# An order of issue written by hand, one broadcast product for four heads, and scores in column halves: one core of a Trainium2

## The chip, the cores and the metric

The kernel runs on one core of one Trainium2 chip. The time is the device time of one execution in microseconds (us), the median of the runs shown. Engines are named as in the profile: PE (TensorE, matrix products; PEld its loads of the stationary operand), DVE (VectorE), ACT (ScalarE), POOL (GpSimd), SP (SyncE, which here issues nearly all transfers).

## The reference, cut to what matters

Three parts follow each other: a gated linear attention over 768 steps for 4 batches of 8 heads with head dimension 40, then two feed-forward layers 320 -> 2048 -> 320 on the 3072 tokens.

```python
for t in range(S):                       # attention, per batch and head
    m_new = np.maximum(f_gate[:, :, t] + m, i_gate[:, :, t])
    f_stab = np.exp(f_gate[:, :, t] + m - m_new)
    i_stab = np.exp(i_gate[:, :, t] - m_new)
    m = m_new
    C = f_stab * C + i_stab * outer(vt, kt)
    n = f_stab * n + i_stab * kt
    y[:, :, t] = sigmoid(o_gate[:, :, t]) * (C @ qt) / max(abs(n @ qt), 1)
x = y, heads side by side                # 3072 x 320
x = relu(x @ w_in) ** 2 @ w_out          # layer 0
return elu(x @ w2_in) @ w2_out           # layer 1, elu(h) = h if h > 0 else exp(h) - 1
```

## The kernel before

The attention is computed in 6 chunks of 128 steps. A unit u is one chunk of one batch (24 in all), and n counts half units of four heads (48 in all). Within a chunk the weights of step s for step t are `exp(a_s - max_t)`, where `a` is the running gate term and `max` its running maximum; scores times these weights give P, and P times the values gives the output. For later chunks the maximum is stored to memory and read back as a broadcast (`mb_load`), masked on POOL (`mask`) and put through the exponential with `a` as the bias (`emit_E`, one ACT instruction for each head). For the first chunk (n = 0 to 7) the whole exponent is built on PE by `m_pe`: one product puts in the causal mask (`identr` by `negmask`), one for each head broadcasts minus the maximum over the 128 rows (a column of the identity `sel`, repeated by a zero step, by `nst`), and one adds `a` (`ast` by `sel`, repeated). `e0` takes the exponential of the 128x512 result in one ACT instruction. Numbers in `nst` and `ast` are held in 64 rows, a high and a low part of 32 rows each, one row for each batch and head.

Scores: `s_pe` for n = 0 to 7 multiplies 40 rows (the head dimension), `scores` does it for the other n; for n = 8 to 15 its operands are plain fp32 with 120 rows, of which 80 are zeros (n < `NPLAIN` = 16), for later n an fp32r form in 120 rows. `emit_P` multiplies with the weights on DVE. `columns` splits a product into two, over the first and last 64 columns of the stationary operand, which write PSUM partitions 0 to 63 and 64 to 127; `pv0` and `values` use it for the values. `state_sum` adds up the state. `evac0`/`evac`, `norm`, `trans`, `x_hi`, `x_lo` bring the output into X, the input of layer 0, for four units at a time.

A weight tile f (16 for each layer) arrives as `raw` and is turned into a high and a low fp32r part by `w_scale`, `w_low`, `w_hi` on ACT and `w_shift`, `w_sign`, `w_add`, `w_lo` on DVE. One step of a layer is one tile of 128 hidden columns for 512 tokens: `mm1` (8 products into h, line 492), `elem` (ACT) and `elem_lo` (DVE), `mm2` (8 products into acc, line 536).

The order of the first part is written out by hand: the string `ORDER` is a list of words, a letter for the task and a number, and each engine gets its instructions in just this order (`manual_schedule`). The letters: Q scores' operands, K keys, values and output gate, q, B, R (weight tile), G, r are loads; m, e, s, p, v, z are maximum's term, exponential, scores, P, values and their copy for n = 0 to 7; k, o, n, t, h, l are the weighting of the keys, the output gate, norm, transposes and the two parts of X for each unit; b, c, d, f, a, H, L are the seven steps of a weight tile (scale, low, shift, sign, add, high part, low part); M, E, S, V, Z, y, Y are the attention of the later chunks; 1, A, F, 2, 3 are the steps of layer 0 (mm1, elem, elem_lo, the first five and the last three products of mm2); g, x, C, U, D are the gates. `i3` puts three products of 512 columns into `dps` (line 657), whose result is never read; 20 of them stand before everything else. With step 20 the string ends and a loop goes on for the rest. `h` has two PSUM buffers; PE's products of `m_pe` use them too.

Of the kernel before, what the change touches and what calls it, by code (L numbers as in the profile page):

```python
# [6 lines left out]
F32 = mybir.dt.float32  # L7
F32R = mybir.dt.float32r
# [32 lines left out]


ORDER = """
R0 Q0 G1 K0 Q1 Q2 K1 Q3 R1 R2 Q4 K2 c0 Q5 Q6 b0 K3 s0 Q7 g1 q4 Q9 m0 o0 k0 K4 Q8 i2 m1 d0 e0 D1 f0 G2 x1 K5 m2
p0 R3 e1 k1 q5 a0 o1 i1 v0 Q11 e2 Q10 H0 i2 m3 r0 z0 G3 L0 i1 m4 c1 e3 i1 s2 b1 e4 i1 m5 p2 b2 d1 i2 v2 f1 e5
d2 R4 i1 m6 o2 k2 z2 a1 f2 i1 m7 H1 c2 L1 i2 s4 e6 k3 R5 a2 o3 i2 s1 p4 H2 L2 i3 v4 p1 i4 s3 o4 B8 B10 B12 i2
v1 p3 o5 i4 s5 B9 z1 n0 c3 i2 v3 p5 b3 z4 i1 t0 z3 d3 i4 s7 e7 n1 h0 l0 i2 s6 p7 b4 f3 i1 C1 i4 v5 p6 R6 U1 a3
k4 b5 i2 t1 k5 B11 z5 d4 M8 H3 n2 i1 v7 h1 E8 i3 v6 l1 M12 c4 f4 M9 i3 t2 B14 E12 z7 M10 R7 z6 d5 i2 S8 n3 h2
E9 Q12 l2 i3 t3 M11 f5 h3 M14 E10 l3 i2 10 a4 E11 g2 11 c5 L3 A0 D2 R8 a5 12 p8 A1 F0 13 b6 F1 c6 S9 d6 f6 H4
20 Q13 H5 p9 R9 30 L4 A2 V4 a6 L5 q6 c7 B16 F2 B13 14 b7 B15 Z4 b8 H6 S10 x2 d8 E14 21 Q14 L6 M16 f8 31 b9 M13  # L50
22 n4 A3 15 d9 K6 M15 A4 d7 f9 16 f7 E13 F3 R10 a7 32 E15 t4 p10 23 k6 F4 H7 33 A5 L7 24 17 c8 F5 h4 R11 a8
b10 l4 34 H8 d10 25 c9 L8 A6 R12 35 f10 18 a9 A7 F6 S11 26 Q15 p11 c10 F7 H9 R13 36 a10 b11 V5 L9 c11 q7 d11
b12 B17 Z5 19 A8 n5 H10 27 o6 A9 37 L10 K7 t5 M17 110 F8 f11 b13 d12 h5 R14 28 a11 f12 H11 C2 38 k7 d13 c12 29
L11 A10 R15 a12 111 f13 c13 U2 F9 S12 H12 a13 b14 39 Q16 p12 c14 210 d14 l5 H13 S13 L12 A11 112 L13 F10 b15
p13 310 o7 d15 A12 V6 F11 f15 q8 f14 B18 y16 113 Z6 E17 E16 211 a14 A13 311 M18 n6 S14 212 Q17 p14 c15 K8 F13
H14 S15 F12 E18 L14 t6 312 p15 h6 114 l6 a15 y17 Y16 V7 H15 k8 A14 q9 L15 Q18 B19 115 Z7 o8 213 n7 A15 313 S16
F14 K9 t7 p16 214 y18 M19 F15 h7 Y17 314 E19 215 l7 Q19 116 Y18 o9 k9 g3 Q20 117 A16 D3 118 A17 F16 119 x3 S17
315 y19 p17 V8 F17 P15 Y19 216 Z8 Q21 B20 A18 120 B21 q10 n8 316 S18 K10 F18 t8 y20 217 p18 h8 Y20 S19 A19 317
M20 121 p19 Q22 l8 M21 y21 F19 E20 V9 Y21 q11 B22 Z9 Q23 218 B23 A20 318 n9 C3 219 A21 U3 K11 319 F20 S20 p20
F21  # L60
"""


def body(tc, qk, qp, kvo, gates, wq, ident_in, qkm_in, out):
# [28 lines left out]
    ident = constp.tile([128, 128], F32, name="ident")  # L93
    msk = constp.tile([128, 1], F32, name="msk")
    msk2 = constp.tile([64, 1], F32, name="msk2")
    sel = constp.tile([64, 32], F32R, name="sel")
    qkm = constp.tile([3 * D, 2], F32, name="qkm")
    one = constp.tile([64, 1], F32, name="one")
    dve.memset(msk[0:64], 0.0)
# [757 lines left out]
```

## Time and profile before

| | |
|---|---|
| median of 3 runs | 836.69 us (836.54 to 837.39) |
| the profiled execution, its own time | 834.66 us |
| its span on the engines | 832.8 us |
| busy: PE, DVE, ACT, POOL | 820.8, 558.4, 543.8, 119.3 us |

Times in the views are counted from the start of the span. The profiled execution is one of its own; its time lies 2.03 us under the median of the runs.

### The profile page before, as it was taken

Reading aid. Unit: us, or ns where it says so; the run is one execution under the profiler, and the core shown is the slowest. Engines: PE = TensorE matmul, PEld = TensorE weight load, DVE = VectorE, ACT = ScalarE, POOL = GpSimd, SP = SyncE. Lnnn points to the kernel's source line nnn. Section 1 sums busy time; section 2 is a strip of 40 time slices with the busy share of each in tenths; the row PEclk is TensorE's granted clock in tenths of the full one; section 3 lists DMA queues with packets and bytes.
Section 4 is the critical chain, followed back from the end, with each engine's and each line's share of the span. In section 5 each row is a group of like instructions: output and inputs, shape, how many; then the busy total and the mean of one; then the engine's idle time right before and its main releaser. Section 6 shows DMA issues by size and latency. Waiting matters only on the chain.

```text
span 832.8 us, 14363 instructions
## 1 busy us (share of the span) xinstructions
PE 820.8 (99%) x5349; PEld 693.3 (83%) x5349; DVE 558.4 (67%) x995; ACT 543.8 (65%) x1012; POOL 119.3 (14%) x195
## 2 busy tenths in 40 slices
PE   9999999999999999999999999999999999999997
PEld 5668788788888888888888879999999899999996
DVE  5799997766667666655449975665655665655554
ACT  5589886766776776678479974555644644655543
POOL 4031101211111111000000011111111111111111
PEclk9999999999999999999999999999999999999999
DMA  8845645754655534561235420110200200000000
GB/s 267 269 140 190 201 129 151 243 153 138 177 137 167 150 110 145 148 190 31 86 101 196 140 89 1 37 47 1 83 1 1 83 1 1 33 1 0 32 1 33
DMA packets 32668, 85.39 MB, mean 103 GB/s; under 512 B 4087, under 2 KB 7895, under 8 KB 32599
## 3 DMA queue, kind: packets, MB, share of 16 engines
q1 hardware_dynamic: 32311, 84.15, 33.2%
q8 instruction: 42, 0.69, 0.4%
q10 hardware_dynamic: 288, 0.33, 0.1%
q14 instruction: 27, 0.22, 0.1%
HBM read 75.73 MB, written 8.73 MB: 101 GB/s over the span
## 4 chain that ended last, share of the span: by engine, by line
PE 84%; ACT 6%; DVE 5%; issue 3%; DMA 2%; POOL 0%; POOLq 0%; DVEq 0%; ACTq 0%; SPq 0%
PE h L492 37%; PE acc L536 35%; PE dps L657 2%; PE pv L323 2%; PE s L312 2%; PE in L323 1%; ACT ct L122 1%; ACT w L144 1%; ACT cu L127 1%; ACT ghi L505 1%; PE in L380 1%; ACT r L504 1%; DVE w L150 1%; ACT r L506 1%; DMA rqk<-qk 1%
## 5 line engine op out<-in xcount | busy, mean ns | idle before, releaser
L492 PE MATMUL h<-xh,w 128*128 128x512 f32 x1152 | 357.8, 393 | 0.4
L492 PEld LDWEIGHTS h<-xh,w 128*128 128x128 f32 x1152 | 216.2, 188 | 46.0 <-DVE w L150 0.8
L520 DVE TENSOR_TENSOR glo<-r,ghi 128x512 fp32r<-128x512 f32 x192 | 135.3, 705 | 161.0 <-ACT r L506 84.6
L536 PE MATMUL acc<-w,ghi 128*128 128x320 f32 x768 | 170.2, 308 | 1.2 <-POOL ghi L515 0.6
L510 ACT ACTIVATE r<-h 128x512 f32<-128x512 f32 x96 | 57.6, 600 | 153.7 <-PE h L492 152.2
L492 PE MATMUL h<-xl,w 128*128 128x512 f32 x384 | 150.9, 393 | 0.2 <-DVE xl L397 0.2
L536 PEld LDWEIGHTS acc<-w,ghi 128*128 128x128 f32 x768 | 132.3, 188 | 9.0 <-POOL ghi L515 0.9
L536 PE MATMUL acc<-ghi,w 128*128 128x512 f32 x480 | 128.2, 396 | 0.0
L536 PE MATMUL acc<-w,glo 128*128 128x320 f32 x384 | 118.8, 309 | 0.2 <-DVE glo L520 0.2
L515 POOL TENSOR_SCALAR ghi<-r 128x512 fp32r<-128x512 f32 x96 | 60.4, 629 | 356.3 <-DVE r L514 263.8
L513 DVE SCALAR_TENSOR_TENSOR ex<-ex,th 128x512 f32<-128x512 f32 x96 | 66.4, 692 | 52.0 <-ACT ex L512 51.4
L536 PEld LDWEIGHTS acc<-ghi,w 128*128 128x128 f32 x480 | 87.2, 188 | 16.8 <-ACT y L563 0.3
L505 ACT ACTIVATE ghi<-r 128x512 fp32r<-128x512 f32 x96 | 60.7, 632 | 47.2 <-PE acc L536 46.3
L536 PE MATMUL acc<-glo,w 128*128 128x512 f32 x288 | 81.7, 392 | 2.1 <-DVE glo L520 2.1
L504 ACT ACTIVATE r<-h 128x512 f32<-128x512 f32 x96 | 56.6, 589 | 40.4 <-PE h L492 40.3
L492 PEld LDWEIGHTS h<-xl,w 128*128 128x128 f32 x384 | 72.1, 188 | 11.4 <-DVE xl L397 0.6
L536 PEld LDWEIGHTS acc<-w,glo 128*128 128x128 f32 x384 | 72.1, 188 | 0.4 <-DVE glo L520 0.4
L514 DVE SCALAR_TENSOR_TENSOR r<-h,ex 128x512 f32<-128x512 f32 x96 | 66.3, 691 | 3.1
L536 PEld LDWEIGHTS acc<-glo,w 128*128 128x128 f32 x288 | 53.6, 188 | 13.7 <-DVE glo L520 2.5
L511 ACT ACTIVATE th<-r 128x512 f32<-128x512 f32 x96 | 61.0, 635 | 2.7
L506 ACT ACTIVATE r<-r 128x512 f32<-128x512 f32 x96 | 60.7, 632 | 2.6
L512 ACT ACTIVATE ex<-r 128x512 f32<-128x512 f32 x96 | 59.2, 616 | 0.0
(104 smaller groups left out, 857.4 us busy)
## 6 DMA issues: line engine op xcount, KB each, us to landing
raw<-wq SPq DMA_DIRECT2D x32, 704.0 KB, 5.5
rqk<-qk SPq DMA_DIRECT2D x32, 480.0 KB, 8.1
kvo<-kvo SPq DMA_DIRECT2D x24, 488.0 KB, 6.7
mb<-negm_dr SPq DMA_DIRECT2D x40, 256.0 KB, 4.0
qp<-qp SPq DMA_DIRECT2D x20, 256.0 KB, 5.6
y_dr<-y SPq DMA_DIRECT2D x18, 256.0 KB, 2.9
out<-y SPq DMA_DIRECT2D x22, 160.0 KB, 1.8
yr<-y_dr SPq DMA_DIRECT2D x12, 256.0 KB, 3.1
```

Source lines behind the costliest of these rows:

```text
L492: lambda i=i, a=a, b_=b_: pe.matmul(h[:, 0:n], lhsT=a, rhs=b_, start=(i == 0), stop=(i == len(seq) - 1))
L504: act.activation(out=r, in_=h, func=AF.Relu)
L505: act.activation(out=hi, in_=r, func=AF.Square)
L506: act.activation(out=r, in_=r, func=AF.Square)
L510: act.activation(out=r, in_=h, func=AF.Relu, scale=-1.0)
L511: act.activation(out=th, in_=r, func=AF.Tanh, scale=0.5)
L512: act.activation(out=ex, in_=r, func=AF.Exp, scale=-1.0)
L513: dve.scalar_tensor_tensor(out=ex, in0=ex, scalar=1.0, in1=th, op0=ALU.add, op1=ALU.mult)
L514: dve.scalar_tensor_tensor(out=r, in0=h, scalar=0.0, in1=ex, op0=ALU.max, op1=ALU.subtract)
L515: pool_.tensor_scalar(out=hi, in0=r, scalar1=1.0, scalar2=1.0, op0=ALU.mult, op1=ALU.mult)
L520: dve.tensor_tensor(out=lo, in0=r, in1=hi.bitcast(F32), op=ALU.subtract)
L536: ops.append(lambda: pe.matmul(o, lhsT=l_, rhs=r_, start=first and st, stop=last and sp_))
```

## The change

Four things are changed. `m_pe`'s four products of 128 columns and 64 rows become one of 512 columns and 128 rows: its moving operand `nst4` holds minus the maximum of all heads in 4 blocks of 128 columns, with zeros where a row's head is not the one of that block, and its stationary operand `selq` picks the four rows of n; `ast` and `sel` get 128 rows too, the lower 64 of them zeros. `nst4` and `selq` are prepared once, with two reductions, a copy and a multiply on DVE and two memsets on POOL. The scores of the first two chunks (n = 0 to 15) go through `columns`. The fillers ahead are 17, not 20. The order is a new one: the tasks are the same, and the fillers in it are 33, not 59. The diff, with the two orders up to somewhat past the first step of layer 0 (word `10`):

```diff
@@ -41,23 +41,22 @@
 ORDER = """
-R0 Q0 G1 K0 Q1 Q2 K1 Q3 R1 R2 Q4 K2 c0 Q5 Q6 b0 K3 s0 Q7 g1 q4 Q9 m0 o0 k0 K4 Q8 i2 m1 d0 e0 D1 f0 G2 x1 K5 m2
-p0 R3 e1 k1 q5 a0 o1 i1 v0 Q11 e2 Q10 H0 i2 m3 r0 z0 G3 L0 i1 m4 c1 e3 i1 s2 b1 e4 i1 m5 p2 b2 d1 i2 v2 f1 e5
-d2 R4 i1 m6 o2 k2 z2 a1 f2 i1 m7 H1 c2 L1 i2 s4 e6 k3 R5 a2 o3 i2 s1 p4 H2 L2 i3 v4 p1 i4 s3 o4 B8 B10 B12 i2
-v1 p3 o5 i4 s5 B9 z1 n0 c3 i2 v3 p5 b3 z4 i1 t0 z3 d3 i4 s7 e7 n1 h0 l0 i2 s6 p7 b4 f3 i1 C1 i4 v5 p6 R6 U1 a3
-k4 b5 i2 t1 k5 B11 z5 d4 M8 H3 n2 i1 v7 h1 E8 i3 v6 l1 M12 c4 f4 M9 i3 t2 B14 E12 z7 M10 R7 z6 d5 i2 S8 n3 h2
-E9 Q12 l2 i3 t3 M11 f5 h3 M14 E10 l3 i2 10 a4 E11 g2 11 c5 L3 A0 D2 R8 a5 12 p8 A1 F0 13 b6 F1 c6 S9 d6 f6 H4
-20 Q13 H5 p9 R9 30 L4 A2 V4 a6 L5 q6 c7 B16 F2 B13 14 b7 B15 Z4 b8 H6 S10 x2 d8 E14 21 Q14 L6 M16 f8 31 b9 M13
-22 n4 A3 15 d9 K6 M15 A4 d7 f9 16 f7 E13 F3 R10 a7 32 E15 t4 p10 23 k6 F4 H7 33 A5 L7 24 17 c8 F5 h4 R11 a8
-b10 l4 34 H8 d10 25 c9 L8 A6 R12 35 f10 18 a9 A7 F6 S11 26 Q15 p11 c10 F7 H9 R13 36 a10 b11 V5 L9 c11 q7 d11
-b12 B17 Z5 19 A8 n5 H10 27 o6 A9 37 L10 K7 t5 M17 110 F8 f11 b13 d12 h5 R14 28 a11 f12 H11 C2 38 k7 d13 c12 29
...
+R0 G1 Q0 K0 Q1 Q2 K1 R1 Q3 Q4 K2 Q5 b0 Q6 K3 c0 s0 Q7 g1 R2 m0 q4 Q8 o0 k0 m1 Q9 e0 d0 s1 D1 x1 p0 Q11 m2 e1
+q5 f0 Q10 v0 K4 p1 e2 k1 R3 m3 o1 z0 G2 a0 K5 v1 e3 r0 i1 s2 G3 z1 n0 H0 m4 c1 i1 s3 b1 L0 i1 t0 e4 p2 m5 o2
+k2 d1 h0 p3 m6 e5 l0 v2 e6 f1 v3 z2 m7 R4 o3 k3 z3 a1 s5 n1 H1 i2 s4 i1 C1 p5 c2 p4 i3 s7 b2 U1 L1 i2 v4 B9 e7
+d2 B8 p7 B10 i2 t1 f2 B12 z4 i2 v5 R5 h1 a2 l1 i2 s6 H2 B11 z5 k4 n2 o4 i2 v7 p6 S8 b3 i1 t2 L2 Q12 i1 v6 c3
+d3 z7 f3 B14 k5 h2 o5 z6 R6 a3 n3 H3 c4 l2 b4 i10 t3 M9 L3 h3 M8 E9 l3 i2 10 M10 d4 E8 g2 M12 11 E12 f4 D2 A0
+p8 R7 a4 12 M11 H4 F0 20 b5 M14 L4 c5 d5 30 A1 f5 S9 13 a5 R8 Q13 p9 b6 F1 A2 21 d6 f6 31 c6 F2 22 b7 R9 a6 32
+H5 d7 V4 c7 f7 q6 H6 L5 R10 A3 B16 14 a7 B13 B15 L6 H7 Z4 15 b8 c8 23 A4 d8 F3 f8 16 b9 L7 R11 M16 A5 d9 33
+M13 F4 17 f9 M15 b10 F5 E10 a8 24 d10 H8 n4 34 c9 25 A6 R12 a9 t4 K6 35 f10 26 L8 H9 h4 S10 L9 b11 18 Q14 p10
+A7 d11 F6 f11 S11 b12 19 F7 Q15 c10 d12 k6 x2 l4 R13 E11 a10 36 f12 27 c11 p11 H10 V5 R14 a11 A8 q7 L10 B17 Z5
+C2 110 A9 n5 37 b13 28 c12 F8 K7 o6 t5 R15 E13 U2 38 F9 M17 d13 S12 A10 a12 29 Q16 p12 f13 39 c13 S13 F10 k7
+h5 210 a13 H11 H12 l5 310 L11 c14 111 H13 L12 b14 L13 b15 112 d14 A11 p13 d15 f14 V6 A12 f15 q8 B18 F11 S14
+a14 113 E14 Q17 Z6 c15 211 E15 p14 M18 311 A13 n6 S15 212 F12 K8 H14 F13 t6 o7 312 L14 E16 114 p15 h6 a15 y16
+l6 213 H15 Y16 k8 A14 V7 L15 Q18 q9 Z7 B19 y17 115 E17 n7 o8 313 E18 214 F14 A15 K9 t7 Y17 S16 314 M19 215 p16
+h7 Q19 y18 l7 116 F15 E19 Y18 k9 o9 117 g3 A16 Q20 118 D3 A17 F16 119 x3 S17 315 y19 p17 V8 F17 P15 Y19 216 Z8
...
 """
 
 
@@ -93,7 +92,8 @@
     ident = constp.tile([128, 128], F32, name="ident")
     msk = constp.tile([128, 1], F32, name="msk")
     msk2 = constp.tile([64, 1], F32, name="msk2")
-    sel = constp.tile([64, 32], F32R, name="sel")
+    sel = constp.tile([128, 32], F32R, name="sel")
+    dve.memset(sel.bitcast(F32), 0.0)
     qkm = constp.tile([3 * D, 2], F32, name="qkm")
     one = constp.tile([64, 1], F32, name="one")
     dve.memset(msk[0:64], 0.0)
@@ -308,6 +308,11 @@
         s = s.rearrange("p (h t) -> p h t", h=4)
         k_, q_ = kS.pop(n), qS[n]
         S_t[n] = s
+        if n < NPLAIN:
+            return [
+                lambda i=i: columns(s[:, i, :], k_[:, i * L:(i + 1) * L], q_[:, i * L:(i + 1) * L], slice(0, L))
+                for i in range(4)
+            ]
         return [
             lambda i=i: pe.matmul(s[:, i, :], lhsT=k_[:, i * L:(i + 1) * L], rhs=q_[:, i * L:(i + 1) * L], start=True, stop=True)
             for i in range(4)
@@ -605,10 +610,8 @@
 
         m = ph.tile([128, 4, L], F32, tag="h", name="h")
         pe.matmul(m, lhsT=identr, rhs=negmask, start=True, stop=False)
-        for i in range(4):
-            r = 4 * n + i
-            pe.matmul(m[:, i, :], lhsT=sel[:, r:r + 1].to_broadcast([64, 128]), rhs=nst, start=False, stop=False)
-        pe.matmul(m, lhsT=ast, rhs=sel[:, 4 * n:4 * n + 4].unsqueeze(2).to_broadcast([64, 4, L]), start=False, stop=True)
+        pe.matmul(m, lhsT=selq[:, n:n + 1].to_broadcast([128, 128]), rhs=nst4, start=False, stop=False)
+        pe.matmul(m, lhsT=ast, rhs=sel[:, 4 * n:4 * n + 4].unsqueeze(2).to_broadcast([128, 4, L]), start=False, stop=True)
         mp_t[n] = m
 
     def s_pe(n):
@@ -616,7 +619,7 @@
         s = s.rearrange("p (h t) -> p h t", h=4)
         t = raw_t.pop(n)
         for i in range(4):
-            pe.matmul(s[:, i, :], lhsT=t[0:D, 1, i * L:(i + 1) * L], rhs=t[0:D, 0, i * L:(i + 1) * L], start=True, stop=True)
+            columns(s[:, i, :], t[0:D, 1, i * L:(i + 1) * L], t[0:D, 0, i * L:(i + 1) * L], slice(0, L))
         S_t[n] = s
 
     def e0(n):
@@ -662,12 +665,19 @@
     pool_.memset(mz, 0.0)
     pool_.affine_select(out=negmask, in_=mz, pattern=[[0, 4], [1, L]], compare_op=ALU.is_ge, fill=NEG, base=0, channel_multiplier=-1)
 
+
+    ast = gc.tile([128, L], F32R, name="ast")
+    selq = gc.tile([128, 8], F32R, name="selq")
+    nst4 = gp.tile([128, TT], F32R, tag="ghi", name="nst4").rearrange("p (h t) -> p h t", h=4)
+    pool_.memset(nst4[64:128].bitcast(F32), 0.0)
+    pool_.memset(ast[64:128].bitcast(F32), 0.0)
+
     plain = [a2.tile([3 * D, 2, 4 * L], F32, tag=tag, name="rqk") for tag in ("rqk", "qks") * 2]
     for x in Cf + plain:
         pool_.memset(x, 0.0)
     early = es.enter_context(ExitStack())
     early.enter_context(tc.manual_schedule(engines={x.engine for x in (pe, act, dve, pool_, sp)}))
-    idle(20)
+    idle(17)
     gate_load(0)
     sp.dma_start(out=ident, in_=ident_in)
     gate(0)
@@ -675,11 +685,16 @@
         act.activation(out=sel[r:r + 32], in_=ident[r:r + 32, r:r + 32], func=AF.Copy)
     act.activation(out=identr, in_=ident, func=AF.Copy)
     aw0, nm0 = aw_t[0]
-    nst = gc.tile([64, L], F32R, name="nst")
-    ast = gc.tile([64, L], F32R, name="ast")
-    for x, y in ((nst, nm0), (ast, aw0[:, 0, :])):
-        act.activation(out=x, in_=y, func=AF.Copy)
-        dve.scalar_tensor_tensor(out=x, in0=x.bitcast(F32), scalar=msk2, in1=y, op0=ALU.mult, op1=ALU.add)
+    nst = gc.tile([64, L], F32, name="nst")
+    sums = gc.tile([128, 12], F32, name="sums")
+    dve.tensor_reduce(out=sums[:, 0:8], in_=sel.bitcast(F32).rearrange("p (n i) -> p n i", i=4), axis=AX.X, op=ALU.add)
+    dve.tensor_reduce(out=sums[:, 8:12], in_=sel.bitcast(F32).rearrange("p (n i) -> p i n", i=4), axis=AX.X, op=ALU.add)
+    dve.tensor_copy(selq, sums[:, 0:8])
+    for x, y in ((nst, nm0), (ast[0:64], aw0[:, 0, :])):
+        act.activation(out=x.bitcast(F32R), in_=y, func=AF.Copy)
+        dve.scalar_tensor_tensor(out=x.bitcast(F32R), in0=x.bitcast(F32), scalar=msk2, in1=y, op0=ALU.mult, op1=ALU.add)
+    own = sums[0:64, 8:12].unsqueeze(2).to_broadcast([64, 4, L])
+    dve.tensor_tensor(out=nst4[0:64], in0=nst.unsqueeze(1).to_broadcast([64, 4, L]), in1=own, op=ALU.mult)
     gate_exp(0)
     for f in gate_cols(0):
         f()
```

## Rows read from the trace of the kernel before

**Rows 1.** The page's first part: busy us (share of the span) xinstructions of each engine.

```profile
PE 820.8 (99%) x5349; PEld 693.3 (83%) x5349; DVE 558.4 (67%) x995; ACT 543.8 (65%) x1012; POOL 119.3 (14%) x195
```

**Rows 2.** Stretches (from:to, length): busy us (instructions) by engine, granted clock, DMA share, GB/s.

```profile
8.15:53.23 45.08, 43.13 (x394) 27.30 (x395) 34.08 (x74) 27.96 (x66) 12.23 (x16) 1.00 0.81 260
53.23:139.90 86.67, 85.39 (x624) 69.43 (x624) 78.11 (x156) 74.38 (x137) 11.32 (x15) 1.00 0.50 156
```

**Rows 3.** The chain that ended last, up to 60 us: start us, us, what.

```profile
1.31 6.84 PE dps L657 x20
...
8.68 1.08 PE acc L619 x8
...
11.59 0.23 PE h L607
11.82 0.59 PE h L610 x4
12.41 0.27 PE h L611
...
13.96 0.32 PE dps L657
...
33.08 0.97 PE dps L657 x4
...
43.25 0.33 DVE num L645
...
53.23 6.87 PE h L492 x29
```

**Rows 4.** DVE's waits before 53 us: us in total, times, longest us.

```profile
DVE mb L318 <- PE acc L619: 3.5, 2, 3.2
DVE num L645 <- PE pv L328: 2.9, 4, 1.4
DVE mb L318 <- PE s L619: 2.9, 1, 2.9
```

**Rows 5.** The same chain as rows 3, from 106 to 116 us.

```profile
106.28 1.84 PE h L492 x8
...
108.81 0.73 PE in L323 x16
...
110.76 2.04 PE h L492 x8
...
114.61 0.91 PE s L312 x8
```

**Rows 6.** The timeline: start us, us, engine, line, instruction, out<-in, shapes, count.

```profile
6.38 0.34 DVE L682 SCALAR_TENSOR_TENSOR ast<-ast,msk,gaw 64x128 fp32r<-64x128 f32 x1
...
6.66 0.63 POOL L663 TENSOR_SCALAR_AFFINE_SELECT negmask<-mz 128x512 fp32r<-128x512 f32 x1
...
10.75 0.21 DVE L193 TENSOR_SCALAR gnm<-gnm 32x128 f32<-32x128 f32 x1
...
12.24 0.68 DVE L318 TENSOR_TENSOR mb<-acc,mb 128x512 f32<-128x512 f32 x1
```

**Rows 7.** The timeline of PE's weight loads, 108.5 to 111 us.

```profile
108.74 0.63 PEld L323 LDWEIGHTS in<-cf,qp 104*64 104x64 f32 x16 [0.36 <-issue]
109.30 1.03 PEld L323 LDWEIGHTS pv<-kvo,mb 128*64 128x64 f32 x32
```

**Rows 8.** Groups of ACT and DVE, 53 to 140 us: xcount | busy us, mean ns | idle.

```profile
L304 ACT ACTIVATE mb<-mb,cols 128x128 f32<-128x128 f32 x35 | 10.9, 392 | 0.0
L122 ACT ACTIVATE ct<-raw 128x704 f32<-128x704 f32 x10 | 8.4, 850 | 0.5 <-ACT mb L304 0.5
...
L150 DVE TENSOR_TENSOR w<-ct,w 128x64 fp32r<-128x64 f32 (+1 forms) x26 | 12.5, 527 | 0.2 <-ACT w L144 0.2
L136 DVE SCALAR_TENSOR_TENSOR ct<-raw,ct 128x704 int32<-128x704 int32 x10 | 10.1, 1025 | 0.0
L131 DVE TENSOR_SCALAR ct<-ct 128x704 int32<-128x704 int32 x10 | 5.2, 525 | 0.1
```

More of the change, by code (lines that the diff above doesn't have):

```diff
@@ L54 @@
[L54 to L58, printed above, removed]
@@ L59 @@
-M20 121 p19 Q22 l8 M21 y21 F19 E20 V9 Y21 q11 B22 Z9 Q23 218 B23 A20 318 n9 C3 219 A21 U3 K11 319 F20 S20 p20
-F21
+R0 G1 Q0 K0 Q1 Q2 K1 R1 Q3 Q4 K2 Q5 b0 Q6 K3 c0 s0 Q7 g1 R2 m0 q4 Q8 o0 k0 m1 Q9 e0 d0 s1 D1 x1 p0 Q11 m2 e1
+q5 f0 Q10 v0 K4 p1 e2 k1 R3 m3 o1 z0 G2 a0 K5 v1 e3 r0 i1 s2 G3 z1 n0 H0 m4 c1 i1 s3 b1 L0 i1 t0 e4 p2 m5 o2
+k2 d1 h0 p3 m6 e5 l0 v2 e6 f1 v3 z2 m7 R4 o3 k3 z3 a1 s5 n1 H1 i2 s4 i1 C1 p5 c2 p4 i3 s7 b2 U1 L1 i2 v4 B9 e7
+d2 B8 p7 B10 i2 t1 f2 B12 z4 i2 v5 R5 h1 a2 l1 i2 s6 H2 B11 z5 k4 n2 o4 i2 v7 p6 S8 b3 i1 t2 L2 Q12 i1 v6 c3
@@ L61 @@
+Q21 B20 A18 120 B21 q10 n8 316 S18 F18 217 K10 y20 p18 t8 A19 Y20 S19 121 M20 p19 Q22 h8 y21 M21 l8 C3 317 U3
+E20 Y21 V9 F19 q11 Q23 Z9 B22 218 B23 A20 318 n9 219 A21 S20 F20 K11 319 p20 F21
 """
```

## The prediction, made before the result

> **What bounds the kernel now.** I read the page's first part first: PE is busy for 99% of the span and no other engine for more than 67% [rows 1]. So the time is PE's work plus PE's gaps, and a step pays only if it shortens what PE executes or the gaps in it. The table by stretches then shows that the kernel is not of one piece [rows 2]. From 53.23 to 139.90 us PE has 1.3 us of gaps in 86.67 while DVE is busy 78.11 and ACT 74.38: three engines near their limits. From 8.15 to 53.23 us PE is "busy" 43.13 of 45.08 us, but part of that is filler: the products into dps, whose result nobody reads. The reader is to see in the chain [rows 3] that up to 43 us every piece is PE's, fillers among them, and that the last ten microseconds before the first real product at 53.23 are DVE's.
>
> A filler costs nothing where PE would have waited. So I looked at who waits in the first stage [rows 4]. DVE's waits in it are 3.5 + 2.9 us for scores and 2.9 us for values, all products of PE; no line says that DVE waits for a transfer or for ACT. So DVE stands behind PE, and PE stands behind the maximum's term and behind fillers. That time can be won.
>
> **The change part by part.**
>
> *Maximum's term (m, eight of them).* Before, one is 0.23 + 0.59 + 0.27 = 1.09 us where it follows a filler; the filler behind such a group shows 0.32 us, where a further one takes (0.97 - 0.32)/3 = 0.217 [rows 3]. So 1.19 each with that 0.10. The four 128-column products take 0.59 for 4 x 128 columns; the new one puts the same 512 columns into one product of 128 rows. Such products take 1.84/8 = 0.23 us [rows 5]: three are 0.69, 0.50 less, 8 x 0.50 = 4.0 us. Bounds: 0.27 each if the operand repeated by a zero step, and not the 64 rows, makes L611's piece longer (3.0 us won), 0.217 each as a filler (4.3). I take 4.0, since the new products are nearest to those of 128 rows.
>
> *Preparation.* DVE gets two reductions, a copy and a 64x512 multiply ahead of the first m. Nearest rows: 0.21 us for the small ones, 0.68 for 128x512 [rows 6]: 1.3 us, after 6.72 us, where the old chain ended (6.38 + 0.34). That is 8.0 us. Hidden: with three fillers fewer, PE leaves the fillers at 8.15 - 0.65 = 7.5 us and has one group of scores (1.08 us) before the first m [rows 3], at 8.6 or later. POOL's memsets add at most 0.8 us (nearest: 0.63 for a pass over 128x512), and the mask that ended at 7.29 ends by 8.1. The second ghi buffer is taken by the new operand until the last m, long before the first elementwise step needs it. Cost zero; without that cover it would be 1.3 us.
>
> *Fillers.* 20 become 17 ahead, 59 become 33 in the order: 29 x 0.217 = 6.3 us of PE.
>
> *Scores in halves.* For n = 8 to 15 one group now takes 0.91 us (8 products of 128 columns) with no extra cost around it; the values and the state's product already go in halves [rows 5]. There the 16 weight loads of the 84-column halves run from 108.74 to 109.30 [rows 7], 0.070 us a pair, so the two halves of a pair run side by side; no row has a pair of 128 columns. Scaled to 128 columns: 0.107 a pair, 8 pairs 0.85 us. So halving wins 0.06 at best. Around them: entering costs 0.73 - 0.56 = 0.17, and the group of eight after the block is 2.04 and not 1.84, 0.20 more. A group in halves between whole products is 1.22, +0.31. In the new order six of the eight stand so (S9 to S13 and S15); S8 and S14 come right behind values and share their switch: 0. Sum +1.9 us. For n = 0 to 7 (1.08 us now [rows 3], already between other shapes): no change, 8 x 0.107 + the same switches. Bounds of this part: 0, if the switch vanishes; and, if 128-column halves did not overlap, 16 x 0.107 + 0.37 = 2.08, +1.17 each for eight (+9.4), and +0.6 each for n = 0 to 7.
>
> The row of the 84-column pairs says that halving only splits one group into two that overlap: 0.85 us. The Trainium skill, "TensorEngine Tiling (Array Packing)", Theoretical Speedup, promises up to 2x where one dimension is at most 64. By that reading a group of scores would fall to 0.46 us, eight of them winning 3.6 us where I count 1.9 lost. The stationary operand is still 128 columns in all, so the row decides here; the same page's Key Properties say that a change of the tiling mode drains the engine, which speaks against these six groups, and the 0.17 and 0.20 us agree.
>
> *Order of issue, first stage.* PE's side: 53.23 - 0.65 (three fillers) - 4.0 - 5.6 (26 fillers) = 43.0 us for the first product of the hidden layer, with its present 2 us of gaps. DVE is late next. It was busy 34.08 us between 8.15 and 53.23 [rows 2]. The new order puts the shift and sign steps of weight tiles 4 and 5 behind that product (2 x (0.525 + 1.025) = 3.1) and takes one w_lo (2 x 0.527 = 1.1) ahead of it [rows 8]: 32.0 us of work in a stretch that I let begin at 8.1 us, about where it begins now (what DVE does there needs the gates' transposes, which follow the first fillers). Of the 9.3 us that DVE waited for PE I leave 4, because values still follow scores and the exponential; none is one bound, 9.3 the other. 8.1 + 32.0 + 4 = 44.1 us, against 53.23: 9.1 us won. The last transposes (t3, behind ten fillers) wait on this same DVE chain.
>
> Loads: the second tile of weights goes earlier, the third behind scores' loads and two kvo, so the third and fourth kvo come 704 KB, some 2.7 us at the 260 GB/s of this stretch [rows 2], sooner; the third weight tile's readers on ACT come late in the new order. POOL now has k4 and k5, which wait for the fifth and sixth kvo, ahead of its part of n2 and n3: if those loads came after n2's input, every microsecond would be n2's and the transposes'. No wait of DVE or PE in rows 4 is for a load, so I put zero.
>
> *Order of issue, after that.* What the first stage no longer does, the next one must: on ACT twelve exponentials (12 x 0.392 = 4.7) and one w_scale (0.85) [rows 8], on DVE 3.1 - 1.1 = 2.0. ACT goes from 74.38 to 79.9 and DVE from 78.1 to 80.1 us within a stretch of 86.67 + 1.9. They still fit, but the slack is what absorbed waits before. PE has two h buffers, so an ACT that lags stalls PE. I take 2 us; bounds 0 and, if ACT keeps all its 12.3 us of idle time, 79.9 + 12.3 - 86.7 = 5.5.
>
> **Sum**, against the profiled execution (span 832.8, its own time 834.66): -9.1 + 1.9 + 2.0 = -5.2, so 829.5. The runs shown have a median of 836.69, 2.03 above the profiled one; on their scale 836.69 - 5.2 = **831.5 us**. From 140 us on nothing is changed, and the shift goes through one to one.
>
> **Rivals.**
> 1. *PE alone decides.* DVE fills its waits fully, the first stage ends at 43.0 (-10.2), later gaps do not grow: -10.2 + 1.9 = -8.3, 828.4 us. For it: DVE waited only for PE. Against: it leaves DVE no idle time of note over 35 us. 0.15.
> 2. *The halves double the rate*, as the skill's page reads: 1.9 + 3.6 better than my sum, 826.0. The 84-column row speaks against it. 0.03.
> 3. *The fillers were waiting time.* DVE's 9.3 us of waits stay whole: 8.1 + 32.0 + 9.3 = 49.4, -3.8 + 1.9 + 2 = +0.1, 836.8, no change. For it: scores and values still alternate with ACT's exponential. Against: PE never idled before 43 us. 0.08.
> 4. *ACT lags after the first stage* and keeps its idle time: -9.1 + 1.9 + 5.5 = -1.7, 835.0; slower only from 7.2 us of added gaps. 0.08 (0.05 of it no change, 0.03 slower).
> 5. *The other side: halves of 128 columns do not overlap.* Place: the scores, s and S. PE's floor in the first stage rises by 8 x 0.6 to 47.8 (3.7 later than 44.1), and 9.4 us are added after: -9.1 + 3.7 + 9.4 + 2 = +6.0, 842.7. It makes the kernel slower once a pair takes about 0.17 us and not 0.107. Against: the 84-column halves in the trace overlap. 0.08.
>
> My forecast, a gain between 2.5 and 7.5 us, has 0.58. What a measurement here can tell from no change is about 0.2%, 1.7 us. Faster: 0.58 + 0.15 + 0.03 = 0.76; same: 0.08 + 0.05 = 0.13; slower: 0.03 + 0.08 = 0.11. Range: from 827.0 (nearly all of rival 1) to 836.5 (nearly all of rivals 3 and 4); it leaves out rivals 2 and 5 and the tails, about 2 in 10. The likeliest case's own range is 829.2 to 834.2.
>
> **What would show it.** In the profile after: an m of three pieces of about 0.23 us; the first h product of L492 near 44 us with DVE's x_lo just ahead of it; scores of n = 9 to 13 near 1.2 us with the neighbour's group about 0.2 longer; PE's gaps between that product and V6 about 3 us. I am wrong if the first product comes at 49 us (rival 3), if scores take 1.7 us or more (rival 5), or if PE waits for ACT's Relu or Square over and over between 44 and 130 us (rival 4). The granted clock, 1.00 in each stretch [rows 2], stayed so over PE's 1.95 us of gaps before 53.23; a fall behind a longer one at t3 would make PE's products there slower and is not in my sum.

## The result and the profile after

The changed kernel takes **828.04 us** (median of 4, 826.77 to 828.86) where the kernel before takes 836.62 (median of 4, 835.37 to 837.39). The ratio is 0.9898 (95% interval 0.988 to 0.9915): faster by 8.6 us, where 5.2 were forecast. The profiled execution took 827.7 us, 7.0 less than that of before (834.66). Where an execution took over 1.5% longer than the fastest of its kernel, the ratios below leave it out.

The page of the changed kernel, its span and the first row of busy times, answers to [rows 1]:

```profile
span 825.9 us, 14524 instructions
...
PE 813.3 (98%) x5424; PEld 689.0 (83%) x5424; DVE 559.6 (68%) x1000; ACT 543.0 (66%) x1012; POOL 120.3 (15%) x197
```

Over the whole kernel PE is still the busiest engine, 98% of the span, with 7.5 us less of work. Its timeline at the start of the stage shows what became of m, the maximum's term:

```profile
7.74 1.09 PE L328 MATMUL acc<-rqk 40*64 40x128 f32 x16
8.76 0.50 PE L612 MATMUL h<-negmask,identr 128*128 128x512 f32 x1
9.10 0.40 PE L613 MATMUL h<-nst,selq 128*128 128x512 f32 x1
9.33 0.38 PE L614 MATMUL h<-sel,ast 128*128 128x512 f32 x1
9.55 0.40 PE L612 MATMUL h<-negmask,identr 128*128 128x512 f32 x1
```

Starts of pipelined products are to be read, not their lengths: 0.23 us from one to the next, 0.69 for a term, as forecast; only the first piece behind the scores takes 0.34. The first term starts at 8.76 us, right behind a group of scores, so its preparation on DVE is hidden.

Then the chain of waits of the same kernel up to 60 us, which answers to [rows 3]:

```profile
5.11 10.14 DMA raw<-wq
15.27 9.96 DMA raw<-wq
...
26.65 8.61 DMA raw<-wq
35.29 0.86 ACT ct L122
...
40.41 0.49 DVE xt L376
...
41.49 1.67 DVE w L150 x2
43.16 0.33 DVE xl L402
```

No piece of it up to here is PE's. The weight loads feed ACT, ACT feeds DVE, and the first products of the hidden layer wait for DVE's x_lo. In the lists of waits, PE's from 8 to 60 us and DVE's before 45 us (us in total, times, longest), the roles are swapped against [rows 4]:

```profile
PE xt L385 <- DVE xt L376: 1.9, 1, 1.9
PE h L497 <- DVE xl L402: 0.8, 1, 0.8
```

```profile
DVE num L648 <- PE pv L333: 1.7, 3, 0.9
DVE ct L131 <- ACT ct L122: 0.9, 1, 0.9
...
DVE mb L323 <- PE s L328: 0.2, 1, 0.2
```

DVE waited 9.3 us for scores and values before and waits 1.9 now. The table by stretches (columns as in [rows 2]):

```profile
8.00:44.00 36.00, 32.66 (x412) 21.82 (x409) 31.42 (x73) 24.67 (x56) 9.87 (x15) 0.99 0.95 293
44.00:130.00 86.00, 85.34 (x670) 67.80 (x670) 80.32 (x156) 76.66 (x145) 13.98 (x17) 0.98 0.54 171
```

The gain can be followed by the starts of PE's products: the first of a step of the hidden layer, counted from 0, and PE's last of all.

| start, us | step 0 | 4 | 8 | 22 | 92 | 100 | last product |
|---|---|---|---|---|---|---|---|
| before | 52.5 | 65.2 | 83.2 | 158.2 | 461.4 | 492.7 | 828.8 |
| changed | 42.3 | 60.9 | 77.2 | 149.9 | 453.1 | 486.4 | 821.7 |

From step 22 on the lead is 8.3 us, to step 92 unaltered. Between steps 96 and 100, at the change of layers, 2.0 us are given back, and 7.1 are left at the end. There PE waits for DVE's elem_lo, 0.5 us longer than before; one row of PE's timeline of the kernel before, then one of the changed kernel and its table of that microsecond:

```profile
484.69 0.98 PE L536 MATMUL acc<-glo,w 128*128 128x512 f32 x3 [2.05 <-DVE glo L520]
```

```profile
476.95 1.65 PE L541 MATMUL acc<-glo,w 128*128 128x512 f32 x3 [2.56 <-DVE glo L525]
```

```profile
477.00:478.00 1.00, 1.00 (x3) 0.81 (x4) 0.50 (x1) 0.81 (x2) 0.32 (x1) 0.50 0.06 14
```

The granted clock reads 0.50 (1.2 GHz of 2.4) behind that gap, from 477 to 480 us, so three products take 1.65 us and not 0.98. Behind the gap before it stayed at 1.00. Two of the experiments below tell the two causes apart by the same steps 96 and 100. In experiment 6 the wait is as long as before, but the clock falls, and the lead shrinks from 8.1 to 6.5 us (step 96 starts at 467.8 where it was 475.9 before, step 100 at 486.2):

```profile
476.61 1.03 PE L541 MATMUL acc<-glo,w 128*128 128x512 f32 x3 [2.06 <-DVE glo L525]
```

```profile
478.00:479.00 1.00, 1.00 (x4) 0.81 (x3) 1.00 (x2) 1.00 (x3) 0.00 (x0) 0.50 0.39 150
```

In experiment 11 the wait is 2.73 us, 0.7 longer than before, and the clock holds: the lead shrinks from 8.8 to 8.1 (467.1 and 484.6). So of the 2.0 us here some 0.5 are the longer wait and about 1.5 the clock, an estimate from these two runs.

### The profile page after: what moved, and what is told of

Its sections match the earlier page's. It is cut to its first block, busy times and chain, and to the rows that moved or that the text cites. A ratio compares the mean times of both kernels' runs of the same rounds, so it can differ in the third digit from the quotient of the medians.

```text
span 825.9 us, 14524 instructions
## 1 busy us (share of the span) xinstructions
PE 813.3 (98%) x5424; PEld 689.0 (83%) x5424; DVE 559.6 (68%) x1000; ACT 543.0 (66%) x1012; POOL 120.3 (15%) x197
## 4 chain that ended last, share of the span: by engine, by line
PE 84%; ACT 4%; DVE 4%; DMA 4%; issue 2%; SPq 0%; POOL 0%; POOLq 0%; DVEq 0%; ACTq 0%
PE h L497 39%; PE acc L541 38%; DMA raw<-wq 3%; PE pv L328 2%; PE s L317 2%; PE in L328 2%; ACT ct L122 1%; ACT cu L127 1%; PE in L385 1%; DVE ct L140 1%; DVE w L150 1%; ACT ghi L510 1%; PE pv L333 0%; DVE glo L525 0%; ACT mb L304 0%
## 5 line engine op out<-in xcount | busy, mean ns | idle before, releaser
L509 ACT ACTIVATE r<-h 128x512 f32<-128x512 f32 x96 | 56.7, 590 | 41.5 <-PE h L497 41.4
```

The lines of the kernel that those rows point to most:

```text
L509: act.activation(out=r, in_=h, func=AF.Relu)
```

## The experiments

**The theories.** *Work*: a product costs the time in which PE executes it, whatever stands around it, so removing fillers and shortening the term win what they occupied (the prediction's sum). *Clock*: in the first stage fillers and the term also decide whether TensorE's clock is granted in full; then the same edits, made alone, can cost more than they win. Times below are medians, ratios are to the kernel before beside it. Unless said otherwise the edit is made in the changed kernel, and all twelve compute the same thing.

**1. Scores of the second chunk whole.** The branch for n < NPLAIN is taken out of `scores`; n = 0 to 7 keep their halves.

```diff
-        if n < NPLAIN:
-            return [
-                lambda i=i: columns(s[:, i, :], ...)
-                for i in range(4)
-            ]
```

> The scores of n = 8 to 15 as whole products again, all else as in the changed kernel. Theory A (switching costs, the halves win nothing): six groups of 1.22 us become 0.91 us, 1.9 us faster than the changed kernel, about 826.1 us. Rival (PE has slack there because ACT and DVE are nearly full, so the halves cost nothing): 828.0 us, no difference; the 1.9 us would turn up as PE's waits between 44 and 130 us.

Measured 827.55 us (5), ratio 0.988 (0.9854 to 0.9905). PE's timeline at one group, in this kernel and in the changed one:

```profile
75.91 1.05 PE L312 MATMUL s<-rqk 120*128 120x128 f32 x8
76.72 0.48 PE L492 MATMUL h<-xh,w 128*128 128x512 f32 x1
...
78.65 1.05 PE L312 MATMUL s<-rqk 120*128 120x128 f32 x8
```

```profile
76.19 1.09 PE L328 MATMUL s<-rqk 120*64 120x128 f32 x16
77.22 0.50 PE L497 MATMUL h<-xh,w 128*128 128x512 f32 x1
...
79.25 0.99 PE L328 MATMUL s<-rqk 120*64 120x128 f32 x14
```

From the group to the next one it takes 78.65 - 75.91 = 2.74 us whole and 3.06 in halves: 0.32 more, where 0.31 was forecast (0.22 of it in the group, 1.03 against 0.81 us, and 0.10 around it). But the six such groups make 0.9 us at step 22 (149.0 against 149.9) and not 1.9, and at the last product 0.2: at the change of layers PE waits 2.93 us in this kernel against 2.56, and the clock falls behind the wait as in the changed kernel. The time is the rival's: halves win nothing here, and what they cost is not to be told from nothing.

**2. More fillers ahead of the hidden layer.**

```diff
-... b4 i10 t3 M9 L3 h3 M8 E9 l3 i2 10 M10 ...
+... b4 i18 t3 M9 L3 h3 M8 E9 l3 i7 10 M10 ...
```

> Eight more fillers ahead of the last transposes and five more behind them, where PE stood idle in the changed kernel (39.1 to 41.05 and 42.0 to 43.55 us) and its granted clock then read 0.5 until about 46.4 us. Theory A (the fall of the clock costs what PE did more slowly in these 3 us): about 1.4 us faster, 826.6 us, and the granted clock reads 1.00 from 36 to 48 us. Rival (DVE and ACT set the pace there, PE's slow products are hidden): 828.0 us. If the fillers delay the transposes: up to 1 us slower.

Measured 826.63 us (4), ratio 0.9874 (0.9848 to 0.9899). In the changed kernel the granted clock is 0.61 to 0.50 from 43 to 46 us, behind the gaps at t3 and x_lo; here it stays at 1.00. That gives PE 1.2 us at step 4 (59.7 against 60.9) and nothing at step 8 (77.3 against 77.2): behind it ACT and DVE set the pace. The 13 fillers cost nothing either; the first product starts 0.6 us later, and the second, at 43.59, finds its operand ready. The median is the 826.6 of theory A, but its executions (825.43 to 827.75) overlap those of the changed kernel, and the profiled ones took 827.75 and 827.70: what the trace shows is the rival's case.

**3. The new products in the old order**, with its 20 + 59 fillers.

```diff
-R0 G1 Q0 K0 Q1 Q2 K1 R1 Q3 Q4 K2 Q5 b0 Q6 K3 c0 s0 Q7 g1 R2 m0 q4 Q8 ...
+R0 Q0 G1 K0 Q1 Q2 K1 Q3 R1 R2 Q4 K2 c0 Q5 Q6 b0 K3 s0 Q7 g1 q4 Q9 m0 ...
-    idle(17)
+    idle(20)
```

> The changed products (maximum's term, halves) in the order of before, with its 20 + 59 fillers. Theory A (the order is most of the gain; in the old one DVE's last ten us decide and the fillers hold PE): the term's 4.0 us come only in part, the halves cost 0.3 us each in seven or eight places (2.3 us): 834 to 838 us, within 0.3% of before. Rival (the cheaper maximum's term is the gain, the order only follows): 4.0 us faster or more, 830 to 832 us. First h product: near 51 us by A, near 49 us by the rival.

Measured 834.73 us (12), ratio 0.9974 (0.9957 to 0.999): a quarter to a third of the gain. The first product starts at 49.6 us, 2.9 sooner than before. The time is theory A's; the first product comes nearer to the rival's 49 than to A's 51.

**4. The old term in the new order.**

```diff
-        pe.matmul(m, lhsT=selq[:, n:n + 1].to_broadcast([128, 128]), rhs=nst4, ...)
-        pe.matmul(m, lhsT=ast, rhs=sel[:, 4 * n:4 * n + 4].unsqueeze(2).to_broadcast([128, 4, L]), ...)
+        for i in range(4):
+            r = 4 * n + i
+            pe.matmul(m[:, i, :], lhsT=sel[0:64, r:r + 1].to_broadcast([64, 128]), rhs=nst.bitcast(F32R), ...)
+        pe.matmul(m, lhsT=ast[0:64], rhs=sel[0:64, 4 * n:4 * n + 4].unsqueeze(2).to_broadcast([64, 4, L]), ...)
```

> The maximum's term with its four products of 128 columns and 64 rows again, in the new order with its fillers and halves. Theory A (each term costs PE 0.5 us more and PE now has only some 3 us of gaps before the first h product): 1 to 4 us slower than the changed kernel, 829 to 832 us, first h product at 43.5 to 46 us. Rival (the first stage waits for loads and DVE, so PE's 4 us vanish in its gaps): 828.0 us, first h product at 42.3 us as in the changed kernel.

Measured 845.33 us (5), ratio 1.01 (1.0077 to 1.0123). Both expectations missed. By work alone this kernel would have lost 8 x 0.50 = 4.0 us of the gain; it loses 17. The table by stretches names the cause, in the column after POOL's. First two rows of the changed kernel, then three of this one:

```profile
12.00:24.00 12.00, 12.00 (x169) 8.82 (x170) 9.94 (x23) 9.30 (x21) 3.56 (x4) 1.00 0.91 261
24.00:36.00 12.00, 12.00 (x165) 7.71 (x164) 10.51 (x26) 5.83 (x12) 1.39 (x3) 1.00 0.96 295
```

```profile
8.00:12.00 4.00, 3.95 (x32) 2.85 (x32) 3.54 (x10) 2.99 (x7) 0.90 (x2) 1.00 1.02 298
12.00:24.00 12.00, 11.53 (x96) 8.54 (x97) 6.28 (x15) 5.53 (x12) 2.50 (x3) 0.55 0.90 267
24.00:36.00 12.00, 12.00 (x87) 8.52 (x86) 3.49 (x8) 3.64 (x9) 1.14 (x2) 0.50 0.97 289
```

From between 13 and 14 us on (0.62 in that microsecond) until between 50 and 51 PE runs at half clock, while it is busy nearly all the time. DVE, which now waits 18.6 us for scores and values, starves behind it, and the first product starts at 61.8 us.

**5. The old term with fillers behind it.** Experiment 4, and `i2` behind each of the eight words m0 to m7.

```diff
-... g1 R2 m0 q4 Q8 o0 k0 m1 Q9 ...
+... g1 R2 m0 i2 q4 Q8 o0 k0 m1 i2 Q9 ...
```

> The old maximum's term in the new order, as in the run before it that took 845 us, and two fillers more behind each of the eight terms (16 in all, 3.5 us of PE). Theory B (the 17 us were TensorE's granted clock, which fell at 13.4 us to half and came back at 50.4; fillers behind the terms keep it up): 829 to 835 us in spite of more work on PE, granted clock 1.00 from 10 to 40 us. Rival (the old term is too long for this order in any case): more fillers make it slower still, 847 us or more.

Measured 835.30 us (median of 7), ratio 0.9966 (0.9935 to 0.9998). Three more executions took 851.4 to 858.5 us at a mean granted clock of 0.968 to 0.976, where the seven have 0.993 to 0.997. No trace of those three is kept: where they lost the clock, and whether the kernel or something else is to blame, is open. In the seven, the sixteen products whose result nobody reads make the kernel 10 us faster than experiment 4. The same stretches:

```profile
12.00:24.00 12.00, 12.00 (x132) 7.79 (x130) 7.26 (x16) 6.60 (x14) 3.02 (x4) 1.00 0.90 266
24.00:36.00 12.00, 12.00 (x144) 7.53 (x143) 8.33 (x19) 5.57 (x12) 0.97 (x2) 1.00 0.97 295
```

PE does more work in them than in experiment 4 (132 products against 96) at a granted clock of 1.00. That is the clock theory's case, for seven executions of ten; work alone asks for 3.5 us more than in experiment 4.

**6. The changed kernel without the 33 fillers in its order** (the 17 ahead stay).

```diff
-... z0 G2 a0 K5 v1 e3 r0 i1 s2 G3 z1 n0 H0 m4 c1 i1 s3 ...
+... z0 G2 a0 K5 v1 e3 r0 s2 G3 z1 n0 H0 m4 c1 s3 ...
```

> The changed kernel without the 33 fillers of its order (the 17 ahead stay). Theory B (what the clock needs here the new terms supply only up to about 23 us; from there to the first h product the fillers hold it): the granted clock reads 0.5 in part of the stretch from 23 to 46 us, 2 to 10 us slower than the changed kernel. Rival (fillers fill waits alone, the chain there is DVE's and the transfers'): 826 to 828 us, first h product at 42 us as before.

Measured 827.46 us (4), ratio 0.9862 (0.9828 to 0.9897): the same as with them, which is the rival's time. Theory B was right on the clock and wrong on what it would cost.

```profile
12.00:24.00 12.00, 12.00 (x181) 9.05 (x179) 10.97 (x24) 9.87 (x24) 3.56 (x4) 1.00 0.89 263
24.00:36.00 12.00, 11.08 (x141) 9.31 (x137) 10.51 (x26) 6.06 (x12) 1.18 (x3) 0.62 0.95 303
36.00:48.00 12.00, 7.68 (x43) 5.45 (x42) 11.47 (x25) 10.09 (x26) 5.89 (x8) 0.67 0.75 256
```

The clock holds through the terms, up to 24 us, and falls later. By then PE has room: DVE is as busy as in the changed kernel (10.51 us from 24 to 36 in both), PE waits 3.5 us for its transposes, and the first product starts at 42.4 us. The lost clock costs nothing here, where PE is not the one waited for; it does at the change of layers of the same run. And the changed kernel could have left its 33 fillers out.

**7. One product of 512 columns, but 64 rows.**

```diff
-        pe.matmul(m, lhsT=selq[:, n:n + 1].to_broadcast([128, 128]), rhs=nst4, ...)
-        pe.matmul(m, lhsT=ast, rhs=sel[:, 4 * n:4 * n + 4].unsqueeze(2).to_broadcast([128, 4, L]), ...)
+        pe.matmul(m, lhsT=selq[0:64, n:n + 1].to_broadcast([64, 128]), rhs=nst4[0:64], ...)
+        pe.matmul(m, lhsT=ast[0:64], rhs=sel[0:64, 4 * n:4 * n + 4].unsqueeze(2).to_broadcast([64, 4, L]), ...)
```

> The four heads in one product of 512 columns, but with the 64 rows that hold numbers and not 128; all else as in the changed kernel. If what counts is the one product for four: PE pays only the change between 128 and 64 rows and back, 0.3 to 0.4 us for each of eight terms, 0 to 3 us slower than 828.0, granted clock 1.00. If the 128 rows are what keeps the clock up: the granted clock falls to 0.5 between 10 and 50 us as with the old term, 835 us or more.

Measured 841.92 us (10), ratio 1.0048 (1.0028 to 1.0068).

```profile
12.00:24.00 12.00, 12.00 (x91) 7.39 (x89) 6.54 (x15) 6.17 (x13) 3.13 (x4) 0.53 0.89 271
24.00:36.00 12.00, 12.00 (x88) 7.62 (x85) 5.21 (x13) 5.88 (x12) 0.24 (x1) 0.50 0.97 297
```

Nothing differs from the changed kernel but the number of rows in two products of each term, all zeros in the half left out, and 13.9 us are lost. Part of that is work, as the first expectation had it; here is the first term, still at full clock:

```profile
9.03 0.50 PE L612 MATMUL h<-negmask,identr 128*128 128x512 f32 x1
9.46 0.50 PE L613 MATMUL h<-nst,selq 64*128 64x512 f32 x1
9.81 0.37 PE L614 MATMUL h<-sel,ast 64*128 64x512 f32 x1
```

By starts it takes 1.08 us (the next one starts at 10.11), where the changed kernel's first term, in the same place, takes 9.55 - 8.76 = 0.79. Eight times 0.29 is 2.3 us; the other 11 to 12 come with the clock. The mean granted clock of its ten executions is 0.975 to 0.980 (0.994 to 0.996 in those of the changed kernel), so this is no accident of one profile. The run does not separate two readings: that 64 rows lose the clock as such, or that the changes between 64 and 128 rows do, in which PE counts as busy.

**8. The kernel before with 29 fillers of its 59.**

```diff
-... k0 K4 Q8 i2 m1 d0 e0 D1 f0 G2 x1 K5 m2 p0 R3 e1 k1 q5 a0 o1 i1 v0 ...
+... k0 K4 Q8 i1 m1 d0 e0 D1 f0 G2 x1 K5 m2 p0 R3 e1 k1 q5 a0 o1 v0 ...
```

> The kernel before with 29 of the 59 fillers in its order, the rest as it was. The prediction's step on fillers (each is 0.217 us of PE, and DVE waits only for PE): the first h product comes 3 to 6 us earlier, 831 to 834 us. Theory B (with the old terms the fillers hold the granted clock): the clock falls to 0.5 within the first 50 us, 5 to 17 us slower than before.

Measured 849.02 us (4), ratio 1.0119 (1.0081 to 1.0158): where 30 x 0.217 = 6.5 us of PE's work were taken out, the kernel takes 11.4 us more than the one before beside it (837.66). First two rows of the kernel before, then two of this one:

```profile
8.00:12.00 4.00, 4.00 (x25) 2.82 (x25) 3.04 (x8) 1.74 (x5) 0.72 (x1) 1.00 1.03 323
12.00:24.00 12.00, 12.00 (x102) 7.51 (x101) 7.38 (x13) 8.38 (x17) 2.36 (x3) 1.00 0.88 289
```

```profile
8.00:12.00 4.00, 4.00 (x25) 2.79 (x24) 3.45 (x8) 2.36 (x5) 0.72 (x1) 1.00 0.99 296
12.00:24.00 12.00, 12.00 (x59) 8.34 (x58) 4.27 (x9) 6.30 (x11) 2.00 (x2) 0.50 0.89 296
```

With the same four microseconds of PE "busy" ahead of it, the clock halves at 12 us; it had held in the kernel before with its fillers. What PE does at half clock is in its timeline, one term:

```profile
16.46 1.11 PE L610 MATMUL h<-nst,sel 64*128 64x128 f32 x4
17.37 0.73 PE L611 MATMUL h<-sel,ast 64*128 64x512 f32 x1
18.04 0.61 PE L657 MATMUL dps<-dr 128*128 128x512 bf16 x1
```

By starts, L610 takes 0.91 us and L611 0.67; in the timeline of the kernel before, by starts at 15.73, 16.23 and 16.59 us, they take 0.50 and 0.36. The kernel before isn't far from this itself: of its 19 executions beside experiments 5 to 8, two took 843.1 and 843.4 us at a mean granted clock of 0.988.

**9 to 11. The change of layers, and a combination.** Number 9 tries to take a weight tile's conversion away from DVE there; 10 is that with experiment 1; 11 is 10 with more fillers ahead of t3 and the first product, and with w_lo of tile 3 (`L3`) moved behind that product.

```diff
-        if last or l == 1 and j == 0 and m % 2 == 0:
+        if last and m not in (13, 14) or l == 1 and j == 0 and m % 2 == 0:
```

```diff
-... b4 i10 t3 M9 L3 h3 M8 E9 l3 i2 10 M10 d4 E8 ...
+... b4 i18 t3 M9 h3 M8 E9 l3 i7 10 M10 L3 d4 E8 ...
```

> The changed kernel, with the weight conversion left out of the steps 13 and 14 of the last sweep of layer 0 (the tiles are converted two steps later, none is dropped). Theory C (part of the gain is given back at the change of layers: PE waits 2.56 us there for DVE's low part, which stands behind conversions, against 2.05 before, and its granted clock then reads 0.5 for some 3 us): the wait shrinks below 0.5 us, 2 to 3.5 us faster than the changed kernel, 824.5 to 826 us. Rival (ACT is simply full there, the work only moves behind the change): 828.0 us.

> The same, with the scores of n = 8 to 15 as whole products too. Theory C (whole scores did bring the first part of the kernel 0.9 us ahead, and the wait at the change of layers took it back): 0.7 to 1.9 us faster than with halves, about 824 us. Rival (halves cost nothing at all): the same time as with halves.

> The same again, and around the first h product: w_lo of the fourth weight tile behind x_lo and not ahead of it, and thirteen more fillers where PE is idle. If DVE's chain sets the first h product: it comes 1.7 us earlier than 43.5 (41.5 to 42.0), and half of that or less is left at the end, since DVE and ACT are nearly full after it: 0.5 to 1 us faster than the run before. Rival (DVE only does the same work later): no difference.

Measured 827.26 (5), 827.05 (4) and 826.45 us (5); ratios 0.9891 (0.9874 to 0.9907), 0.9891 (0.9874 to 0.9908) and 0.9885 (0.9867 to 0.9903). Numbers 9 and 10 missed what theory C expected (826 us or less, and about 824). Number 9 says nothing on its question: PE waits 2.58 us at the change of layers, DVE's instructions ahead of it stand as they did, with the same durations, because so late in the kernel their order is the planner's. In number 11 PE is busy for 36.00 of the 36 us from 8 to 44. The product that waits for x_lo was expected at 41.5 to 42.0 us and starts at 43.2 (43.55 in the changed kernel), so DVE's chain was hardly shortened. A row of its table by stretches, and PE's wait at the change of layers:

```profile
44.00:130.00 86.00, 83.06 (x614) 67.59 (x613) 80.56 (x157) 76.42 (x145) 12.72 (x16) 1.00 0.54 171
```

```profile
476.58 0.96 PE L536 MATMUL acc<-glo,w 128*128 128x512 f32 x3 [2.73 <-DVE glo L520]
```

It is the fastest of all by its median, but its 5 executions (824.98 to 827.37) overlap those of the changed kernel, which it beats by 1.6 us across two comparisons: likely better, not proven. In the profiled executions it leads the changed kernel by 0.5 us at step 92 and by 1.8 at step 100 (484.6 against 486.4); what came between is the clock, which behind this wait stayed at 1.00. Such differences are those between executions of one kernel: number 9's one execution at a mean granted clock of 1.000 took 825.05 us, its other four, at 0.995 to 0.998, 826.87 to 828.01. The 44-to-130 row is the useful one: with the clock at 1.00 PE has 2.9 us of gaps there, where the changed kernel shows 0.7 and a lower clock.

**12. Four products of 128 columns, but 128 rows.**

```diff
-        pe.matmul(m, lhsT=selq[:, n:n + 1].to_broadcast([128, 128]), rhs=nst4, ...)
+        for i in range(4):
+            r = 4 * n + i
+            pe.matmul(m[:, i, :], lhsT=sel[:, r:r + 1].to_broadcast([128, 128]), rhs=nst4[:, i, :], ...)
```

> The changed kernel with minus the maximum put in by four products of 128 columns again, but on 128 rows (each head's block of nst4), all else as in the changed kernel. PE executes what it does there with three more instructions for each of the eight terms. Theory (the rows used, 128 against 64, decide whether the granted clock holds in the new order with its few fillers): granted clock 1.00 from 12 to 36 us, first product of the hidden layer at 42 to 44 us, 826.5 to 830 us. Rival (the width of the product decides: only products of 512 columns hold it): granted clock near 0.5 in most of 16 to 44 us as with the old term in the new order, first product after 55 us, 840 us or more. A third case, rows and width both count: clock half in part of 12 to 44 us, first product between 45 and 55 us, 831 to 839 us.

Measured 829.28 us (5), ratio 0.9892 (0.9874 to 0.991). Four of the executions took 826.60 to 830.10 us at a mean granted clock of 0.994 to 1.000, as the changed kernel does. The fifth, the profiled one, took 838.16 at 0.986:

```profile
12.00:24.00 12.00, 12.00 (x97) 9.39 (x97) 5.75 (x14) 5.38 (x11) 1.95 (x3) 0.50 0.90 262
24.00:36.00 12.00, 12.00 (x114) 9.30 (x115) 6.01 (x15) 5.57 (x13) 1.46 (x2) 0.69 0.98 292
36.00:48.00 12.00, 12.00 (x187) 8.11 (x183) 11.00 (x25) 5.54 (x13) 1.90 (x4) 1.00 0.52 172
```

So rows, or the changes of them, decide more than width: on 64 rows all fifteen executions of experiments 4 and 7 lost the clock, on 128 rows four of five kept it with products as narrow as the old ones, going by the mean clock of each. But it is nearer to the edge: the profiled execution, with its first product at 52.75 us, is the third case of the expectation, rows and width both counting; what tipped this one execution is not settled (PE had waited 1.22 us for ACT just ahead, at 6.7 us).

## Why the prediction was right, point by point

**The time** lay in the range, with the forecast sign: 828.0 for 831.5. The gain of 8.6 us is more than the 2.5 to 7.5 of the forecast's own case, and the time is nearer to rival 1's 828.4 than to the forecast. Against the profiled execution the sum was -5.2 and -7.0 came; the last 1.7 us are the scale. I carried the 2.03 us by which that execution lay under its median over to the changed kernel, and its profiled execution lies 0.3 under.

**The term and its preparation** held: 0.69 us, first term at 8.76.

**The first stage** was to gain 9.1 us, its end at 44.1 set by DVE. The 53.23 that it starts from, called the first real product, is the second of the kernel before, which waits for x_lo; the first started at 52.48. In the changed kernel the second starts at 43.55: 9.7 gained, by that wait. DVE was to work 32.0 us from 8.1 and wait 4; from 8 to 44 us it works 31.42 and idles 4.6. Rivals 1 and 3 put the end at 43.0 and 49.4; the chain, DVE's and not PE's, decides against the first, whose other half, that later gaps do not grow, nearly came true (below). The zero for loads was near enough: the chain runs through the weight loads, but their readers cost DVE 0.9 us.

**Scores in halves** cost what was worked out, 0.32 against 0.31 us a group. For n = 0 to 7 a group takes 1.02 us by starts (7.74 to 8.76) for 1.08, no dearer, as forecast. Rivals 2 and 5, half the price and double the price, are refuted. As a term of the sum +1.9 was too much: 0.9 at step 22, and at the end nothing that these runs can tell.

**The term that was mis-sized** is the pair "+1.9 + 2.0" behind the first stage. From the second product to step 22 the changed kernel gives back 9.68 - 8.35 = 1.3 us and not 3.9; 0.9 of it are the halves, which leaves 0.4 for the 2.0. In the stretch to 130 us PE has 0.7 us of gaps, not 3.3: the gap of ACT and DVE is there (2.9 us in experiment 11, 2.0 in experiment 2, against 1.3 in [rows 2]), but in the changed kernel PE ran part of it at half clock instead of waiting, which costs the same (experiment 2 gives that clock back and is no further at step 8). The fall of the clock behind t3 that the prediction left out of its sum came, and was free. Rival 4 did not come about: from 44 to 130 us no wait of PE is for ACT.

**"The shift goes through one to one"** from 140 us on held to step 92 and failed at the change of layers, where 2.0 us are given back, of which 0.8 come again after it. About 1.5 of the 2.0 is a fall of the clock, which the sum had nowhere.

**The reason behind "That time can be won" was incomplete**, and that it did no harm to the number is luck: the change happened to bring the rows on which the clock held. The prediction priced a filler at 0.217 us of PE's time and nothing else. Experiment 8 shows that this is false of the kernel before: half of its fillers taken out cost 11 us. Experiments 4 and 7 show it of the new order: without the 128 rows it is slower than the kernel before (by 7.8 and 4.3 us). The parts don't add up. Beside the kernel before (837.52), the new products in the old order win 2.8 us (experiment 3), the old term in the new order loses 7.8 (experiment 4), and together they win 8.6; the zero rows that the change adds to the term are what lets its order do with few fillers, or with none (experiments 6 and 7). A sum that prices each edit by rows of a kernel at full clock can't see this: priced in that way, experiment 4 was expected at 829 to 832 us and took 845.3.

## What to carry to other kernels

Before taking filler products out of a stage that is a chain of short waits, read the granted clock stretch by stretch and ask what holds it once they are gone. Try products on all 128 rows there, with zeros if need be: in this kernel a term then took 0.79 us and not 1.08, the clock held, and 14 us were won. Price an edit together with the ones it depends on; here the new products alone won 2 to 3 us and the new order alone lost 7.8. And look at what stands at the end of the gain: what was won early met a wait on another engine and a fall of the clock at the change of layers, and a seventh of it was gone at the end (8.3 us to 7.1).

## What the runs showed of the hardware

The granted clock fell to 1.2 GHz with no idle gap of PE before it: in experiment 8 PE is busy 4.00 of 4.00 us from 8 to 12, and at 0.50 from 12 on, up to 48 us, at "100% busy" throughout. What differs from the kernel before, at 1.00, is how many of the products are fillers of 128 rows among products of 40 and 64 rows. The Trainium skill, "TensorE: Matmul & The Clock Gate", Why this matters for your kernels, ties a mid-kernel fall to idle gaps of PE between bursts; experiments 4, 7 and 8 don't agree with that as the only cause. Behind real gaps the fall is not sure either: at the change of layers the clock was 0.50 after 2.06 us in experiment 6 and 2.56 in the changed kernel, and 1.00 after 2.05 in the kernel before and 2.73 in experiment 11. Why is open.
